# A hand-planned instruction order, replanned with one more dependence and two longer products

## The chip, the core and the metric

The kernel runs on one core of a Trainium2 chip. The core has four compute engines that each work through a queue of their own in order: TensorE (PE in the profile, its weight loads PEld), VectorE (DVE), ScalarE (ACT) and GpSimd (POOL); SyncE (SP) only issues DMAs here. An instruction waits, and everything behind it on its engine with it, until semaphores say that its data are there and that the tile it writes is free. The metric is the device time of one execution in microseconds (us).

## What is computed

Two stages in float32. The first is an attention with sketched features, for 4 batches of 4 heads, 1088 positions, 32 dimensions; S1 and S2 are 8 x 32:

```python
a = einsum('rd,bhsd->bhsr', S1, x); b = einsum('rd,bhsd->bhsr', S2, x)
phi(x) = a (outer) b, reshaped to 64 features
kv = einsum('bhsf,bhsd->bhfd', phi(k), v);  z = sum over s of phi(k)
attn = einsum('bhsf,bhfd->bhsd', phi(q), kv) / (einsum('bhsf,bhf->bhs', phi(q), z) + 1e-6)
```

The second takes its 4352 x 128 result x through a network with a rational activation:

```python
h = x @ w_in                      # 128 -> 2048
P = a0 + a1*h + a2*h**2 + a3*h**3
Q = 1 + |b0|*|h| + |b1|*h**2
out = (P / (Q + 1e-6)) @ w_out    # 2048 -> 128
```

## The kernel before, in words

**The attention.** For each batch `keys` transposes k on DVE (L415, L417, into `kT`), multiplies it on PE with the sketches S (L435, into PSUM), copies one half of the result on ACT (L440, `b_sk`), forms the features on DVE (L443, `k_p`) and sums them against v on PE (L454); ACT keeps the result (L473, `kvz`). `queries` does the same for q in pieces of up to 384 positions: DVE transposes (L498, `qT`), and then one of two ways. In the direct way, used for the first two pieces of batch 0, PE multiplies `qT` with SAB, the sketches already repeated for all 64 features: L520 with SAB0 and later L520 with SAB1, into other columns of the same PSUM tile. ACT copies the SAB0 half (L525 or L528, into `a_all`), and DVE multiplies the SAB1 half by the copy (L532 or L535). In the spread way, used for all other pieces, PE makes the plain sketches (L548), ACT copies them (L553, `sk_sb`), SP writes them to DRAM and reads them back repeated (`sk_d`, then `a_all` and `b_all`), and DVE multiplies (L556). Either way PE then multiplies by `kvz` (L589), DVE divides (L598, L602, L605, `x_tok`), PE transposes (L611), and ACT puts the result into `xT` (L618).

**The network.** 4352 tokens are cut into tiles of 256 or 512, each of 16 blocks of 128 hidden features, and the blocks into 29 units of up to 6 blocks (3072 columns). In a unit PE forms h in chunks of 1024 columns (L691) in two PSUM tiles that take turns, ACT takes each chunk out of PSUM (L695), and DVE and ACT compute on the whole unit: DVE |h| (L706), b0 + b1|h| (L711 on DVE or L713 on ACT), its product with |h| (L716); ACT the logarithm (L719) and the exponential of its negative, 1/Q (L722); DVE h/Q (L731) and so on (L734, L737, L740, L749, L752), with a linear term on DVE (L726) or on ACT (L728), and a1 added on DVE (L744) or on ACT (L746). The digit of `MODES` says how many terms of P go through the output matrix separately. In mode 4 there are four terms, 1/Q, h/Q, h^2/Q and h^3/Q, each with a copy of w_out scaled by a0 to a3, and no linear term. In mode 3 there are three, and the linear term a2 + a3*h is multiplied in (L728 or L726, then L737). PE adds the terms up in PSUM (L787, against `w_out`); DVE transposes the sums out (L799) and DMAs store them (L811). The five scaled copies of w_out are made at the start (L391, L393 on ACT; L395, L397 on DVE).

**The order.** The work is cut into 976 steps, each a few instructions on one engine. Every step has a number in `PLACE`; the steps are issued in the order of these numbers, so the table is the order of every engine's queue at once. It comes from a planner outside the kernel; the costs, ranks and slacks that the step calls still carry have no effect here. `ON_ACT` lists the steps that could go to DVE or ACT and go to ACT. `FILLS` gives zero products (L321: an `idle` tile of zeros times itself, 256 columns) ahead of some places. A step's `after` list is only compared with the places; what an instruction waits for follows from the tiles that it reads and writes. Two tiles each named att, out and h are all of PSUM, and 16 tiles t hold the units' columns; each is given in turn to whoever has the next place.

Of the kernel before, what the change touches and what calls it, by code (L numbers as in the profile page):

```python
# [20 lines left out]
def kernel(  # L21
# [38 lines left out]
    PE, DVE, ACTE, POOL, SP = "PE", "DVE", "ACT", "POOL", "SP"  # L60
# [27 lines left out]
    def step(eng, cost, fn, rank, after=(), uses=(), land=None, early=0.0, behind=None, slack=0.0):  # L88
        s = Step()
        s.eng = (ACTE if len(steps) in ON_ACT else DVE) if isinstance(eng, dict) else None  # L90
        s.fn, s.uses = fn, list(uses)
        s.after = [a for a in list(after) + [behind] if a is not None]
        s.place = PLACE[len(steps)]
        for b in s.uses:
            b.left += 1
        steps.append(s)
        return s
# [18 lines left out]
    def act(n, extra=0.0):  # L116
        return 0.04 + 0.000835 * n + extra

    def d_one(n):
        return 0.066 + 0.00104 * n  # L120
# [4 lines left out]
    def d_four(n, ptr):  # L125
# [17 lines left out]
    FILL = 1  # L143
    LATE = 6.96
    Q0B_RANK = -194.15
    GET_SLACK = 1.2
    S_SLACK = (0.0, 1.0)
    V_SLACK = 0.99
    GAP = 0.2
    START = 4.9  # L150
    Q0_PRE = -151.2
    K1_RANK = 0.47
    MODES = '43242333333243333233444244424'
    FIRST_PER = 4
    LAST_PER = (8, 8, 8, 4, 3, 1)
    K0_PARTS = ((0, 1), (1, 4), (4, 6), (6, 8), (8, 9))
# [2 lines left out]
    AB_RANK = -145.0  # L159
# [3 lines left out]
    PERS = (6,)  # L163
    N_T = 16
    PLACE = (
# [48 lines left out]
    )  # L214
    ON_ACT = (
        25, 26, 29, 31, 32, 33, 328, 342, 344, 379, 454, 478, 502, 535, 612, 636, 669, 688, 693, 744, 878,
        889, 914, 932, 951, 953, 960,
    )
    FILLS = {7: 15, 22: 4, 70: 1, 77: 1}
    NW = 5 if '4' in MODES else 3  # L220


# [74 lines left out]
    ab_in = []  # L297
# [71 lines left out]
    st = step(DVE, 0.15, mk_rep, -210, after=s_l)  # L369
# [4 lines left out]
    ab_ps = Buf("out")  # L374
# [1 line left out]
    def mk_ab():  # L376
        nc.tensor.matmul(ab_ps.t[:, 0:6], lhsT=ones, rhs=ab_row, start=True, stop=True)

    st = ab_st = step(PE, 0.11, mk_ab, AB_RANK, after=ab_in, uses=[ab_ps])
    ab_l = step(ACTE, 0.2, lambda: nc.scalar.copy(out=a_sb, in_=ab_ps.t[:, 0:4]), -100, after=[st], uses=[ab_ps])  # L380
    babs = step(ACTE, 0.2, lambda: nc.scalar.activation(out=b_abs, in_=ab_ps.t[:, 4:6], func=ACT.Abs), -100, after=[st], uses=[ab_ps])

# [106 lines left out]
    def queries(b, qb, q_l, c0, c1, rank, how, pre=None, pre2=None, apart=False, early=0.0, size=1):  # L489
# [12 lines left out]
        if how == "direct":  # L502
# [32 lines left out]
                    nc.vector.tensor_mul(out=av(hp), in0=half(hp, n, 2 * n), in1=av(hp))  # L535

            st = step(PE, 0.57 * n / 256, lambda: sketches((0,)), rank if pre is None else pre, after=[tr, sab[0]], uses=[qT] + pair)
            s2 = step(PE, 0.57 * n / 256, lambda: sketches((1,)), rank if pre2 is None else pre2, after=[tr, sab[1]], uses=[qT] + pair)
            st = step(ACTE, act(2 * n) + 0.02 * apart, copies, rank, after=[st], uses=pair + [a])
            ft = step(DVE, d_one(2 * n) + 0.07 * apart, features, rank, after=[st, s2], uses=pair + [a])  # L540
        else:
            sk, c, d, a, bb = (Buf(z) for z in ("att", "sk_sb", "sk_d", "a_all", "b_all"))
# [323 lines left out]
```

## Time and profile before

| | us |
|---|---|
| runs | 266.0, 266.1, 266.26 (median 266.1) |
| the profiled execution | 265.84 |
| its span, first to last instruction | 264.1 |
| granted TensorE clock in the profile | 1.00 |
| PE's last product begins | 259.9 |
| DVE's last instruction ends | 260.7 |
| ACT's last instruction ends | 258.3 |

A row of the timeline gives the start, the duration, the engine, the line, the operation with output and inputs, and how many instructions were merged. In brackets stands how long the engine had been idle, and what ended that. Neighbours on one engine overlap by some 0.1 us in their records, so two rows' starts tell better than a duration what an instruction costs its queue.

### The profile page before, as it was taken

What the parts mean: (1) busy time and instruction counts of PE and PEld (TensorE: products, weight loads), DVE (VectorE), ACT (ScalarE), POOL (GpSimd) and SP (SyncE); (2) the same over time, 40 slices, a digit from 0 to 9 for tenths busy, and PEclk for the clock granted to TensorE, in tenths of its full rate; (3) what the DMA queues carried; (4) which work ended last, traced back from release to release, by engine and by line L of the source; (5) the groups of instructions that cost most, each with busy time, mean ns of one, the idle gap of its engine ahead of it and who ended that gap; (6) DMA issues with size and microseconds to landing.
All of it is one profiled execution on the core that took longest, in us unless ns stands there. A gap on an engine that the chain in (4) does not pass through costs nothing.

```text
span 264.1 us, 4201 instructions
## 1 busy us (share of the span) xinstructions
PE 254.8 (96%) x1641; PEld 141.1 (53%) x1659; DVE 252.4 (96%) x293; ACT 248.5 (94%) x209; POOL 2.7 (1%) x25
## 2 busy tenths in 40 slices
PE   8999999999999999999999999999999999999994
PEld 5767646554544654454444554444444466565683
DVE  3889999999999999999999999999999999999994
ACT  2779999999999999999999999999999999999991
POOL 4000000000000000000000000000000000000000
PEclk9999999999999999999999999999999999999999
DMA  7969344800425347005102530300010110030032
GB/s 199 338 193 241 79 134 128 242 32 0 97 70 178 93 132 163 4 7 129 34 2 80 104 87 21 55 0 0 0 22 2 25 18 0 0 46 0 0 55 40
DMA packets 29063, 20.13 MB, mean 76 GB/s; under 512 B 19316, under 2 KB 24948, under 8 KB 29044
## 3 DMA queue, kind: packets, MB, share of 16 engines
q1 hardware_dynamic: 28352, 19.24, 29.2%
q10 hardware_dynamic: 692, 0.62, 0.8%
q8 instruction: 13, 0.21, 0.4%
q14 instruction: 6, 0.05, 0.1%
HBM read 16.65 MB, written 3.21 MB: 75 GB/s over the span
## 4 chain that ended last, share of the span: by engine, by line
ACT 51%; PE 30%; DVE 10%; issue 8%; POOL 0%; ACTq 0%; POOLq 0%
PE h_ps L691 14%; ACT ln L719 13%; ACT t L722 13%; ACT t L695 11%; PE out_ps L787 7%; ACT t L728 6%; ACT t L713 3%; DVE t L734 2%; DVE t L737 2%; PE att_ps L589 1%; DVE t L731 1%; PE att_ps L548 1%; DVE t L716 1%; PE att_ps L321 1%; PE att_ps L435 1%
## 5 line engine op out<-in xcount | busy, mean ns | idle before, releaser
L691 PE MATMUL h_ps<-xT,w_in_sb 128*128 128x512 f32 (+1 forms) x320 | 127.2, 534 | 1.2 <-ACT xT L618 0.7
L787 PE MATMUL out_ps<-t,w_out 128*128 128x512 bf16 (+1 forms) x480 | 97.8, 344 | 1.9 <-issue 1.1
L691 PEld LDWEIGHTS h_ps<-xT,w_in_sb 128*128 128x128 f32 x320 | 58.8, 190 | 45.4 <-issue 33.3
L787 PEld LDWEIGHTS <-w_out 128*128 128x128 bf16 x498 | 47.2, 98 | 49.5 <-issue 17.9
L695 ACT CAST t<-h_ps 128x1024 bf16<-128x1024 f32 (+1 forms) x69 | 69.4, 1053 | 0.5 <-PE h_ps L691 0.4
L719 ACT ACTIVATE ln<-t 128x3072 f32<-128x3072 bf16 (+4 forms) x29 | 65.5, 2257 | 0.3 <-DVE t L716 0.2
L722 ACT ACTIVATE t<-ln 128x3072 bf16<-128x3072 f32 (+4 forms) x29 | 65.4, 2254 | 0.2
L731 DVE TENSOR_TENSOR t<-t,t 128x3072 bf16<-128x3072 bf16 (+4 forms) x29 | 40.4, 1397 | 0.0
L716 DVE TENSOR_TENSOR t<-t,t 128x3072 bf16<-128x3072 bf16 (+4 forms) x29 | 40.4, 1392 | 0.0
L728 ACT ACTIVATE t<-t,a_sb 128x3072 bf16<-128x3072 bf16 (+2 forms) x13 | 33.3, 2574 | 0.4 <-PE out_ps L787 0.4
L734 DVE TENSOR_TENSOR t<-t,t 128x3072 bf16<-128x3072 bf16 (+3 forms) x23 | 32.7, 1425 | 0.1
L706 DVE TENSOR_SCALAR t<-t 128x3072 uint16<-128x3072 uint16 (+4 forms) x29 | 22.4, 773 | 0.6 <-ACT t L695 0.4
L711 DVE TENSOR_SCALAR t<-t,b_abs 128x3072 bf16<-128x3072 bf16 (+3 forms) x24 | 22.3, 928 | 0.0
L737 DVE TENSOR_TENSOR t<-t,t 128x3072 bf16<-128x3072 bf16 (+1 forms) x13 | 21.6, 1661 | 0.0
L589 PEld LDWEIGHTS att_ps<-kvz,a_all 128*64 128x64 f32 x288 | 9.9, 137 | 4.2 <-issue 2.3
L589 PE MATMUL att_ps<-kvz,a_all 128*64 128x66 f32 x288 | 11.3, 225 | 0.0
L752 DVE TENSOR_TENSOR t<-t,t 128x1024 bf16<-128x1024 bf16 (+3 forms) x10 | 11.2, 1124 | 0.0
L556 DVE TENSOR_TENSOR a_all<-a_all,b_all 128x768 f32<-128x768 f32 (+2 forms) x11 | 9.6, 871 | 0.0
L713 ACT ACTIVATE t<-t,b_abs 128x2048 bf16<-128x2048 bf16 (+3 forms) x5 | 9.0, 1809 | 0.1
L443 DVE TENSOR_TENSOR k_p<-att_ps,b_sk 128x768 f32<-128x768 f32 x9 | 8.5, 949 | 0.0
L454 PEld LDWEIGHTS att_ps<-v_sb,k_p 128*64 128x64 f32 x216 | 6.8, 138 | 2.1 <-issue 1.4
L740 DVE TENSOR_TENSOR t<-t,t 128x3072 bf16<-128x3072 bf16 (+3 forms) x6 | 7.7, 1282 | 0.0
(75 smaller groups left out, 145.9 us busy)
## 6 DMA issues: line engine op xcount, KB each, us to landing
a_all<-sk_d SPq DMA_DIRECT2D x6, 384.0 KB
b_all<-sk_d SPq DMA_DIRECT2D x12, 192.0 KB
kq<-in_k_dram SPq DMA_DIRECT2D x3, 544.0 KB
kq<-in_q_dram SPq DMA_DIRECT2D x3, 544.0 KB
a_all<-sk_d SPq DMA_DIRECT2D x4, 320.0 KB
b_all<-sk_d SPq DMA_DIRECT2D x8, 160.0 KB
v_sb<-in_v_dram SPq DMA_DIRECT2D x4, 288.0 KB
v_sb<-in_v_dram SPq DMA_DIRECT2D x4, 256.0 KB
```

Source lines behind the costliest of these rows:

```text
L589: nc.tensor.matmul(nd.t[x:x + 64, o:o + 2 * KW], lhsT=(av(c)[:, o0 + x:o0 + x + 64] if how == "direct" else q_p.t[:, c * n + o0 + x:c * n ...
L691: nc.tensor.matmul(h.t[:, cols[x] - cols[x0]:cols[x + 1] - cols[x0]], lhsT=w_in_sb[:, f * 128:(f + 1) * 128], rhs=xT[:, xpos(t0):xpos(t0) ...
L695: nc.scalar.copy(out=hh.t[:, cols[x0]:cols[x1]], in_=h.t[:, 0:cols[x1] - cols[x0]])
L706: nc.vector.tensor_scalar(out=u.t[:, :n].bitcast(U16), in0=hh.t[:, :n].bitcast(U16), scalar1=0x7FFF, scalar2=None, op0=AX.bitwise_and)
L716: nc.vector.tensor_mul(out=y.t[:, :n], in0=w.t[:, :n], in1=u.t[:, :n])
L719: nc.scalar.activation(out=ln.t[:, :n], in_=y.t[:, :n], func=ACT.Ln, bias=1.0 + 1e-6)
L722: nc.scalar.activation(out=r.t[:, :n], in_=ln.t[:, :n], func=ACT.Exp, scale=-1.0)
L728: nc.scalar.activation(out=p.t[:, :n], in_=hh.t[:, :n], func=ACT.Identity, scale=a3, bias=a2)
L731: nc.vector.tensor_mul(out=s.t[:, :n], in0=hh.t[:, :n], in1=r.t[:, :n])
L734: nc.vector.tensor_mul(out=(hh if mode == 3 else p).t[:, :n], in0=hh.t[:, :n], in1=s.t[:, :n])
L737: nc.vector.tensor_mul(out=hh.t[:, :n], in0=p.t[:, :n], in1=hh.t[:, :n])
L787: nc.tensor.matmul(o[0].t[:, :bl[x][1]], lhsT=w_sb[y_][:, bl[x][2], :], rhs=src.t[:, cols[x]:cols[x + 1]], start=(o[1] == 1), stop=(o[1] = ...
```

## The change

`PLACE` is new nearly throughout. Beside it five things differ:

```diff
-    GET_SLACK = 1.2
+    GET_SLACK = 1.15
-    MODES = '43242333333243333233444244424'
+    MODES = '43242333333243333233444244423'
-        0, 3, 1, 8, 4, 5, 10, 2, 9, 18, 13, 71, 16, 17, 11, 6, 7, 14, 19, 21, 15, 29, 33, 30, 80, 46, 91,
+        2, 3, 0, 15, 4, 5, 7, 1, 16, 22, 10, 66, 23, 21, 8, 6, 11, 12, 19, 18, 13, 26, 27, 32, 79, 41, 101,
...
-        25, 26, 29, 31, 32, 33, 328, 342, 344, 379, 454, 478, 502, 535, 612, 636, 669, 688, 693, 744, 878,
-        889, 914, 932, 951, 953, 960,
+        25, 27, 29, 31, 32, 33, 328, 342, 344, 379, 454, 478, 502, 535, 612, 636, 669, 688, 693, 744, 878,
+        889, 914, 932, 951, 953, 960, 965,
-    FILLS = {7: 15, 22: 4, 70: 1, 77: 1}
+    FILLS = {11: 15, 14: 3, 63: 1, 78: 1}
...
-    st = ab_st = step(PE, 0.11, mk_ab, AB_RANK, after=ab_in, uses=[ab_ps])
+    st = ab_st = step(PE, 0.38, mk_ab, AB_RANK, after=ab_in, uses=[ab_ps])
...
-            s2 = step(PE, 0.57 * n / 256, lambda: sketches((1,)), rank if pre2 is None else pre2, after=[tr, sab[1]], uses=[qT] + pair)
             st = step(ACTE, act(2 * n) + 0.02 * apart, copies, rank, after=[st], uses=pair + [a])
+            s2 = step(PE, 0.57 * n / 256, lambda: sketches((1,)), rank if pre2 is None else pre2, after=[tr, sab[1], st], uses=[qT] + pair)
```

In instructions: the last unit (256 columns) goes from mode 4 to mode 3, which adds one L728 on ACT and takes away one L787; four zero products ahead of the first key products become three; of the w_out copy scaled by a1, ACT makes the other half than before, and DVE the half that ACT made. All else is order. At the start, PE's order was L520 with SAB0, L520 with SAB1, then the key products of the later parts (L435, L454); it becomes L520 with SAB0, L435 twice, one L454, then L520 with SAB1. On ACT, L525 now comes ahead of the w_out copy L393 instead of behind it. On SP, the first half of w_in now comes ahead of the k of batch 1, and some loads and puts exchange places. Behind the start, DVE's and PE's queues differ in most places, ACT's in fewer.

94 rows, old and new, of the table PLACE are left out of this document.

## The prediction

> **What bounds the kernel.** The profiled execution took 265.84 us: a span of 264.1 and 1.7 around it. The median of the runs shown is 266.1, 0.26 more, so I work from 265.84 and add 0.26 at the end. I read the page's busy times first, then its slices, the chain that ended last, and the timeline of 0 to 62 us engine by engine.
>
> ```profile
> PE 254.8 (96%) x1641; PEld 141.1 (53%) x1659; DVE 252.4 (96%) x293; ACT 248.5 (94%) x209; POOL 2.7 (1%) x25
> ...
> PE   8999999999999999999999999999999999999994
> ...
> DVE  3889999999999999999999999999999999999994
> ACT  2779999999999999999999999999999999999991
> ...
> ACT 51%; PE 30%; DVE 10%; issue 8%; POOL 0%; ACTq 0%; POOLq 0%
> ```
>
> Three engines are full at once, and the chain hops between all three, so no work of one hides behind another for long. What an order can change is idle time alone. DVE's idle time: 4.34 before its first instruction, rows of 0.55, 0.15, 0.30, 0.54, 0.21 and 0.18 up to 20 us, then only 0.25, 0.19, 0.20, 0.41 and 0.36 in the other 240 us. Behind 20 us there is 1.4 to win on DVE, before it about 1.9, and no more. The start looks like this:
>
> ```profile
> 6.73 0.70 PE L520 MATMUL att_ps<-qT,SAB 64*128 64x256 f32 x4
> 7.89 0.97 PE L520 MATMUL att_ps<-qT,SAB 64*128 64x256 f32 x4 [0.46 <-ACT a_all L528]
> 8.62 0.76 DVE L535 TENSOR_TENSOR a_all<-att_ps,a_all 128x256 f32<-128x256 f32 x2 [0.55 <-PE att_ps L520]
> 9.63 1.15 ACT L391 ACTIVATE w_out<-ln,a_sb 128x1024 bf16<-128x1024 f32 x1
> 12.54 1.05 ACT L393 CAST w_out<-ln 128x1024 bf16<-128x1024 f32 x1
> 13.48 0.59 ACT L525 COPY a_all<-h_ps 128x512 f32<-128x512 f32 x1
> 14.12 0.70 PE L520 MATMUL h_ps<-qT,SAB 64*128 64x256 f32 x4 [0.62 <-ACT a_all L525]
> 15.30 0.29 ACT L553 COPY sk_sb<-att_ps 128x160 f32<-128x160 f32 x1 [1.22 <-PE att_ps L548]
> ```
>
> The reader is to see that PE waits twice for the copies of the first query products (0.46 and 0.62), although they lie in other columns of the same PSUM tile: the dependence is real already, and the changed step list only names it. DVE (0.55) and ACT (1.22) wait behind the same places.
>
> **The start.** In the changed order PE does key products while the copies run. On before's rows: three zero products instead of four let the first key products begin at about 5.59 (5.80 less one spacing of 0.21). The L520 pair of 6.73 comes at about 6.5, its copies end at about 7.9, and PE meanwhile does the L435 and L454 groups that stood at 8.79 to 9.5, so the wait of 0.46 is covered by that work. ACT's L391 is now asked for at about 8.1. Its row started at 9.63 without a wait, so its data came somewhere between; if as late as 9.63, the small copy behind it and a DVE product stay where they were, and at 11 us the gain is only 0.2 to 0.3. It comes back: ACT's L393 (0.94 from start to start) no longer stands ahead of L525, which can run at about 12.45 instead of 13.48. So the 0.62 goes, the L520 of 14.12 comes at 13.15, L532 at 14.1 instead of 14.95, and the first L691 at 15.65 instead of 16.53. L691 waits for its half of w_in_sb; SP now issues that ahead of the k of batch 1, one 0.5 MB load earlier. ACT's first L695 then starts at 17.6 instead of 18.56. DVE by 20 us is about 1.05 ahead, ACT 0.95, PE 0.88. **Start: -0.9.** Bounds: -0.25 (the L391 wait is not made good) to -1.2.
>
> The loads and the spread of the later queries move in SP's queue, some behind puts that wait for ACT. On before's rows each has at least 5.7 us between its last forerunner and its use (the q of batch 2 least, as before), and the second half of b_all, now behind the next puts, about 5. I cost this at nothing; without that cover it would be up to 2.8, the longest wait for b_all in SP's own list.
>
> **The middle.** The ACT order is nearly unchanged up to 60 us; DVE's and PE's are not, and two edits spend the gain:
>
> ```profile
> 43.25 1.93 ACT L695 CAST t<-h_ps 128x1024 bf16<-128x1024 f32 x2
> 44.35 1.75 DVE L740 TENSOR_TENSOR t<-t,t 128x3072 bf16<-128x3072 bf16 x1
> 46.10 1.07 DVE L726 TENSOR_SCALAR t<-t,a_sb 128x3072 bf16<-128x3072 bf16 x1
> 51.59 0.51 ACT L618 COPY xT<-att_ps 128x384 f32<-128x384 f32 x1
> 52.16 3.70 PE L691 MATMUL h_ps<-xT,w_in_sb 128*128 128x512 f32 x8 [0.40 <-ACT xT L618]
> 56.62 0.96 DVE L706 TENSOR_SCALAR t<-t 128x3072 uint16<-128x3072 uint16 x1 [0.25 <-ACT t L695]
> ```
>
> At 44.35 DVE did L740, and L726, which needs the last L695 of 43.25 (ended 45.18), came at 46.10, 0.92 later than its data. The changed order has L726 ahead of L740, so DVE asks at 44.35 less its gain of 1.05, 43.3, while ACT's data, 0.95 earlier, come at about 44.25. **DVE waits about 0.95** and has then nothing left of its gain. What is queued behind it: L706, L598 and L740, and through them the next L719. At 52 us the copy L618 moves behind one more L695 (0.90 from start to start), so in spite of ACT's gain it still ends at about 52.1; PE, there 0.24 further in its own work than before, asks at 51.5 and **waits about 0.65 instead of 0.40**. So at 53 us DVE is at 0, PE at -0.24, ACT at -0.95. Then ACT's gain pays: the 0.25 at 56.62 is a wait for ACT's L695 and goes. **DVE at 57 us: -0.25.**
>
> From 60 to 250 us the orders differ throughout. I compared, for each L719 with its L716, each L731 with its L722 and each L695 with its L691, how much work stands ahead of it on its own engine and on the other, by the rows' spacings, before and after. The tightest pairs are alike: ACT has at most 4.40 us less work ahead of an L719 than DVE has through its L716, 4.27 after; DVE at least 4.25 more ahead of an L731 than ACT through its L722, 4.14 after; PE at least 9.11 more ahead of the L691 that reuses a PSUM tile than ACT ahead of its L695, 8.88 after. One pair is worse, the third last L695 (by 0.8 against its L691), where ACT has 2 us to spare to the end. So I expect waits of the same size as before's, at other places. The waits of before behind 57 us that can go are 0.19, 0.20, 0.41 and 0.36 on DVE (1.16 in all), and ACT's lead, which DVE's waits use up, allows 0.70 of it. Bounds: 0 and -0.70; I take half, **-0.35**. PE's products change kind 175 times instead of 180; what one change costs beyond its work is between 0 and 0.16 (the "issue" waits in PE's rows), so 0 to -0.8 on PE, taken as 0, since DVE and ACT are as full.
>
> **The end.** The last unit (256 columns) goes from mode 4 to mode 3: one L787 of 0.11 us less, one L728 on ACT more, about 0.5 (the 256-column L713 took 0.60, 0.51 from start to start). ACT was through at 258.30 and DVE's last product at 259.87, so the 0.5 delays L746 by that much, and L749 behind it, only if ACT's lead is gone. Taken as 0; bounds -0.1 and +0.5.
>
> **Sum:** the start's 0.9 is spent on DVE at L726, -0.25 remains at 57 us, -0.35 comes behind it, 0 at the end: -0.6, so 265.24 for a profiled execution and **265.5** as a median.
>
> **A rule that speaks against fewer zero products.**
>
> ```profile
> 1.29 3.41 PE L321 MATMUL att_ps<-idle 128*128 128x256 bf16 x15
> ...
> 250.90 9.30 PE L787 MATMUL out_ps<-t,w_out 128*128 128x256 bf16 x82 [0.27 <-ACT t L722]
> ```
>
> The zero products are 256 columns wide, as the last L787 are, and take 0.21 apart (3.41 less the last one's own 0.42, over 14), those 0.11: TensorE runs at half rate at the start, though the profile's granted clock reads 1.00 from the first slice on. The L435 of 5.80 (0.69 for 16) run at the rate of later ones, so the full rate came by then, 4.7 us after the first zero product. If the fourth zero product were needed for that, and the half rate lasted as long again, PE's rows from 5.8 to 10.5 would take twice as long: up to 4.5 us, of which 1.0 is covered by waits that go; half of it, as DVE and ACT are still idle there 2 of 5 us, gives 1.8 against a gain of 0.6, so 267.3. Against it: in the changed order PE is at work from 5.59 on, so nothing idles for the want of it.
>
> The Trainium skill ("TensorE: Matmul & The Clock Gate", Part 1) says that the array starts at half clock and is released after a window of about 3.4 us of sustained activity that runs freely, counted in time and not in products. By that rule the removed product costs nothing while other products take its place, and by a rule that counted products it would; the spacings of 0.21 and 0.11 agree with its two rates, and no run so far shows its window.
>
> **Rivals.**
> 1. *The start's gain lasts.* If ACT's evacuations come early enough that L726 and L691 wait less, 0.9 stays, and fewer changes of kind give 0.2: 264.7, median **265.0**. For it: ACT is 0.95 ahead. Against: L726 stands ahead of its data by more than that.
> 2. *The gain is given back.* The waits move and sum to before's: 265.84, median **266.1**. For it: three engines above 94%, any one that loses 0.9 sets the end. This is also what is left if the step list's new dependence changes nothing but names.
> 3. *ACT becomes the last engine, and slower.* At 132 us the changed order puts an L691 0.45 us ahead of the end of the L695 that frees its PSUM tile, which stands behind an L728 of 2.85; at before's 208.78 the same kind of wait was 0.39. With ACT's lead PE doesn't notice. If ACT has lost its lead by then (its L719 at 71 us has only 0.09 to spare against DVE, which stands at -0.25), PE loses 0.45 there and the added L728 its 0.5 at the end: 265.84 + 0.95 = 266.8, median **267.05**. It decides if ACT's lead at 130 us is under 0.2 and the start's gain is gone with it.
> 4. *The half rate lasts*, 267.3, median **267.55**.
>
> **Chances.** Forecast 0.31, rival 1 0.23, rival 2 0.30, rival 3 0.13, rival 4 0.03. What a measurement of this kernel can tell from no change is about 0.2%, 0.53 us. Faster by more: most of the forecast's case (0.26 of 0.31, as -0.6 is near the bound) and rival 1, 0.49; within it: rival 2 and the rest of the forecast, 0.35; slower: 0.16. The range reaches from rival 1 with the start's larger bound (264.6) to the lower part of rival 3 (266.7). The likeliest case's own range is 265.1 to 265.9.
>
> **What would show it.** The first L691 at 15.5 to 15.8, and no 0.46, 0.55, 0.62 or 1.22 in the start's rows; if the first L691 is later than 16.2, the start is wrong. A wait of 0.7 to 1.2 in front of DVE's first L726 of 3072 columns, for L695; if it is under 0.3, rival 1. PE waiting 0.5 to 0.8 for L618 near 51 us. DVE's idle behind 20 us: 1.0 to 1.8 in all, for before's 1.4. A wait of PE for L695 near 131 us and an ACT that ends less than 1 us ahead of DVE speak for rival 3. Zero products and first key products further than 0.11 and 0.06 apart after 6 us speak for rival 4.

## The result and the profile after

The changed kernel takes **265.5 us** (median of 10 runs, 265.03 to 266.51), the kernel before 266.17 (10 runs, 265.87 to 266.46): a ratio of 0.9975, interval 0.9963 to 0.9987, that is 0.67 us less. The profiled execution took 265.17, its span is 263.4, and the column of the granted clock reads 1.00 throughout. The forecast of 265.5 was met; not all of its steps were, as will be seen.

Busy times and the chain that ended last, from the page of the changed kernel:

```profile
PE 255.6 (97%) x1657; PEld 140.5 (53%) x1657; DVE 252.4 (96%) x293; ACT 249.2 (95%) x210; POOL 2.8 (1%) x25
...
PE 49%; ACT 31%; DVE 11%; issue 5%; DMA 3%; DVEq 0%; ACTq 0%
```

PE now has the larger share of the chain (49% for 30%), and a load has entered it (DMA 3%). Of the kernel before, two rows serve as marks, the first product of the network and the last transpose:

```profile
16.53 1.99 PE L691 MATMUL h_ps<-xT,w_in_sb 128*128 128x256 f32 x8
260.24 0.45 DVE L799 STREAM_TRANSPOSE out_sb<-out_ps 128x256 f32<-128x256 f32 x1 [0.36 <-PE out_ps L787]
```

The timeline of the changed kernel, start and end:

```profile
5.58 0.69 PE L435 MATMUL h_ps<-S,kT 128*64 128x64 f32 x16 [0.35 <-DVE S L355]
9.45 1.15 ACT L391 ACTIVATE w_out<-ln,a_sb 128x1024 bf16<-128x1024 f32 x1 [1.33 <-DMA ln<-in_moe_w_out_dram]
10.71 0.42 DVE L443 TENSOR_TENSOR k_p<-h_ps,b_sk 128x256 f32<-128x256 f32 x1 [0.63 <-ACT b_sk L440]
11.19 0.45 PE L454 MATMUL out_ps<-v_sb,k_p 128*64 128x64 f32 x8 [0.56 <-DVE k_p L443]
12.75 0.59 ACT L525 COPY a_all<-h_ps 128x512 f32<-128x512 f32 x1 [0.28 <-PE h_ps L520]
13.46 0.70 PE L520 MATMUL h_ps<-qT,SAB 64*128 64x256 f32 x4
14.64 0.29 ACT L553 COPY sk_sb<-att_ps 128x160 f32<-128x160 f32 x1 [0.25 <-PE att_ps L548]
15.81 1.99 PE L691 MATMUL h_ps<-xT,w_in_sb 128*128 128x256 f32 x8
259.53 0.45 DVE L799 STREAM_TRANSPOSE out_sb<-out_ps 128x256 f32<-128x256 f32 x1 [0.48 <-PE out_ps L787]
```

The waits of 0.46, 0.55 and 0.62 are gone, and of the 1.22 ahead of L553 0.25 is left. In their place ACT's L391 stands 1.33 until the first half of w_out has landed; behind it stands the small copy L440, and so L443 (0.63) and L454 (0.56). L525 no longer stands behind L393, and the first L691 comes at 15.81 instead of 16.53, **0.72 earlier**. The last L799 begins at 259.53 instead of 260.24, 0.71 earlier. Within 0.01, nothing was won or lost in the 244 us between.

### The profile page after: what moved, and what is told of

Its sections match the earlier page's. It is cut to its first block, busy times and chain, and to the rows that moved or that the text cites. A ratio compares the mean times of both kernels' runs of the same rounds, so it can differ in the third digit from the quotient of the medians.

```text
span 263.4 us, 4224 instructions
## 1 busy us (share of the span) xinstructions
PE 255.6 (97%) x1657; PEld 140.5 (53%) x1657; DVE 252.4 (96%) x293; ACT 249.2 (95%) x210; POOL 2.8 (1%) x25
## 4 chain that ended last, share of the span: by engine, by line
PE 49%; ACT 31%; DVE 11%; issue 5%; DMA 3%; DVEq 0%; ACTq 0%
PE h_ps L691 24%; PE out_ps L787 16%; ACT t L695 9%; ACT ln L719 9%; ACT t L722 7%; ACT t L728 4%; PE att_ps L589 3%; DVE t L734 3%; DVE t L731 3%; PE att_ps L454 2%; DMA ln<-in_moe_w_out_dram 2%; DVE t L752 2%; DMA kq<-in_k_dram 1%; PE att_ps L548 1%; DVE t L716 1%
## 5 line engine op out<-in xcount | busy, mean ns | idle before, releaser
L691 PE MATMUL h_ps<-xT,w_in_sb 128*128 128x512 f32 (+1 forms) x320 | 127.4, 534 | 1.1 <-ACT t L695 0.7
L787 PE MATMUL out_ps<-t,w_out 128*128 128x512 bf16 (+1 forms) x497 | 100.7, 346 | 0.5 <-DVE t L731 0.4
L691 PEld LDWEIGHTS h_ps<-xT,w_in_sb 128*128 128x128 f32 x320 | 58.8, 190 | 44.5 <-issue 32.5
L787 PEld LDWEIGHTS <-w_out 128*128 128x128 bf16 x497 | 47.2, 98 | 50.3 <-issue 18.9
L695 ACT CAST t<-h_ps 128x1024 bf16<-128x1024 f32 (+1 forms) x69 | 69.2, 1041 | 0.7 <-PE h_ps L691 0.5
L728 ACT ACTIVATE t<-t,a_sb 128x3072 bf16<-128x3072 bf16 (+3 forms) x14 | 34.2, 2442 | 0.0
L706 DVE TENSOR_SCALAR t<-t 128x3072 uint16<-128x3072 uint16 (+4 forms) x29 | 22.6, 778 | 0.6 <-ACT t L695 0.5
L737 DVE TENSOR_TENSOR t<-t,t 128x3072 bf16<-128x3072 bf16 (+2 forms) x14 | 21.9, 1572 | 0.0
L752 DVE TENSOR_TENSOR t<-t,t 128x1024 bf16<-128x1024 bf16 (+2 forms) x9 | 10.9, 1214 | 0.0
L556 DVE TENSOR_TENSOR a_all<-a_all,b_all 128x768 f32<-128x768 f32 (+2 forms) x11 | 9.7, 878 | 0.0
L443 DVE TENSOR_TENSOR k_p<-att_ps,b_sk 128x768 f32<-128x768 f32 x9 | 8.5, 952 | 0.4 <-ACT b_sk L440 0.3
L454 PEld LDWEIGHTS att_ps<-v_sb,k_p 128*64 128x64 f32 x216 | 6.8, 138 | 2.7 <-issue 1.8
```

Source lines behind the costliest of these rows:

```text
L691: nc.tensor.matmul(h.t[:, cols[x] - cols[x0]:cols[x + 1] - cols[x0]], lhsT=w_in_sb[:, f * 128:(f + 1) * 128], rhs=xT[:, xpos(t0):xpos(t0) ...
L695: nc.scalar.copy(out=hh.t[:, cols[x0]:cols[x1]], in_=h.t[:, 0:cols[x1] - cols[x0]])
L706: nc.vector.tensor_scalar(out=u.t[:, :n].bitcast(U16), in0=hh.t[:, :n].bitcast(U16), scalar1=0x7FFF, scalar2=None, op0=AX.bitwise_and)
L728: nc.scalar.activation(out=p.t[:, :n], in_=hh.t[:, :n], func=ACT.Identity, scale=a3, bias=a2)
L787: nc.tensor.matmul(o[0].t[:, :bl[x][1]], lhsT=w_sb[y_][:, bl[x][2], :], rhs=src.t[:, cols[x]:cols[x + 1]], start=(o[1] == 1), stop=(o[1] = ...
```

## The experiments

The most useful reading of the study splits each profile at the first L691, the first product of the network. The sixth column is the length from there to the last L799; the profiled time is 5.59 to 5.66 more than the start of that L799 in every row. "L391" is the start of the first copy of w_out; each ratio is against runs of the kernel before on the same chip in the same set.

| kernel | first L391 | first L691 | L691 less L391 | last L799 | length | median | ratio to before (interval) |
|---|---|---|---|---|---|---|---|
| before | 9.63 | 16.53 | 6.90 | 260.24 | 243.71 | 266.17 | |
| changed | 9.45 | 15.81 | 6.36 | 259.53 | 243.72 | 265.5 | 0.9975 (0.9963-0.9987) |
| e1 changed start | 10.20 | 16.55 | 6.35 | 260.25 | 243.70 | 265.77 | 0.9991 (0.9974-1.0008) |
| e2 changed rest | 9.68 | 16.58 | 6.90 | 260.27 | 243.69 | 266.31 | 1.0008 (0.9998-1.0018) |
| e3 no zero products | 9.51 | 18.02 | 8.51 | 261.68 | 243.66 | 267.25 | 1.0044 (1.0031-1.0057) |
| e4 small copy first | 10.04 | 15.98 | 5.94 | 259.76 | 243.78 | 264.8 | 0.9959 (0.9947-0.9970) |
| e5 L740 first | 9.45 | 15.80 | 6.35 | 259.39 | 243.59 | 265.23 | 0.9974 (0.9962-0.9985) |
| e6 last unit mode 4 | 9.37 | 15.72 | 6.35 | 259.49 | 243.77 | 265.62 | 0.9992 (0.9963-1.0020) |
| e7 SAB1 alone | 9.41 | 16.31 | 6.90 | 260.01 | 243.70 | 266.06 | 1.0008 (0.9988-1.0028) |
| e8 L525 alone | 9.56 | 16.20 | 6.64 | 259.91 | 243.71 | 265.64 | 0.9979 (0.9957-1.0000) |
| e9 DVE +0.9 | 9.38 | 15.74 | 6.36 | 259.55 | 243.81 | 265.56 | 0.9980 (0.9967-0.9993) |
| e10 ACT +0.9 | 10.27 | 16.62 | 6.35 | 261.33 | 244.71 | 266.46 | 1.0013 (1.0003-1.0024) |
| e11 PE +1.0 | 10.64 | 17.00 | 6.36 | 261.54 | 244.54 | 266.35 | 1.0012 (0.9997-1.0027) |
| e12 e4, second L391 later | 10.16 | 16.14 | 5.98 | 260.24 | 244.10 | 265.33 | 0.9972 (0.9956-0.9989) |

**e1 and e2: start and rest apart.** The two orders hold the same steps in their first 128 places but for two, so each start can be joined to the other's rest.

```
e1: PLACE = changed order[0:128]   + order of before for the other steps   (last unit mode 4)
e2: PLACE = order of before[0:128] + changed order for the other steps     (last unit mode 3)
```

> The first 128 places (about 22 us) in the changed order with its zero products, all steps behind them in the order of before, last unit in mode 4. Theory A, the start's gain lasts (0.4 us of DVE idle and 0.7 us of PE and ACT position won in the first 20 us): median 265.5 to 265.7, that is 0.45 to 0.7 under before. Theory B, the start's gain is spent at the later waits and the gain of the change comes from the order behind 22 us: within 0.2 of before (266.2). Theory C, both parts give about half: 265.75 to 265.95.

> The first 128 places in the order of before with its zero products, all steps behind them in the changed order, last unit in mode 3. Theory A: within 0.2 of before (266.2). Theory B: 265.4 to 265.7. Theory C: 265.75 to 265.95. If start and rest only work together, because the rest was laid out for engines that are ahead by the changed start, then this one is slower than before, 266.4 to 267.

The changed rest behind the old start (e2) gains nothing: 243.69 for 243.71, and 1.0008. Theory A holds there, and B falls. The median of e1, 265.77, lies in C's range, but its interval, from 0.9974 to 1.0008, reaches over A's range and over no gain at all. So it does not decide between A and C; that e2 gained nothing speaks against C, and the profile of e1 does too: the old rest behind the changed start takes the same 243.70, and the first L691 stands 6.35 behind L391, as in the changed kernel. It came late because the load did:

```profile
10.20 1.15 ACT L391 ACTIVATE w_out<-ln,a_sb 128x1024 bf16<-128x1024 f32 x1 [1.99 <-DMA ln<-in_moe_w_out_dram]
```

SP's queue is the same in e1 and the changed kernel up to this load, so 9.45 and 10.20 are two landings of the same order. In the nine profiles that have the changed start with its zero products L391 began between 9.37 and 10.64, each time behind a wait for this load.

**e7 and e8: the two parts of the start apart**, each on the kernel before.

```
e7 PE : L520(SAB0), L435, L435, L454, L520(SAB1), L435, L454 ...   was L520(SAB0), L520(SAB1), L435, L435, L454 ...
e7 DVE: L443, L443, L535                                           was L535, L443, L443
e8 ACT: L553, L525, L393                                           was L553, L393, L525
```

> The kernel before with one part of the change alone: the L520 with SAB1 stands behind three key products' groups and one L454 on PE, and L535 behind two more L443 on DVE, as in the changed kernel. Theory, ACT's L391 waits for its data and holds the key chain up, so that PE's gain of 0.5 at 8 us is lost again by 11 us and L393 is still ahead of L525: first L691 within 0.15 of 16.53, median 266.0 to 266.3. Rival, the removed waits of 0.46 and 0.55 are the gain of the change: first L691 at 15.9 to 16.1 and 265.5 to 265.8.

> The kernel before with the other part alone: ACT's L525 ahead of the w_out copy L393. Theory, this is what gives the start's gain: the wait of 0.62 of PE's L520 goes, first L691 at 15.7 to 16.0 instead of 16.53, median 265.4 to 265.7, as much as the whole change. Rival, the start's gain is eaten by DVE's and PE's next waits in the order of before (the 0.54 before L532 goes, and the loads of w_in and k come no earlier): 265.9 to 266.2.

e7: no gain in time (1.0008), as the theory said; the first L691 came at 16.31, 0.07 further from 16.53 than expected, because L391 could begin at its landing, 9.41. The length of 6.90 behind L391 is that of before: PE's early products don't shorten it. e8: the wait of 0.62 goes and some time with it (0.9979, with an interval that just reaches 1), but L691 comes at 16.20, not at 15.7 to 16.0. In e8's timeline:

```profile
12.85 0.59 ACT L525 COPY a_all<-h_ps 128x512 f32<-128x512 f32 x1 [0.29 <-PE h_ps L520]
13.49 0.70 PE L520 MATMUL h_ps<-qT,SAB 64*128 64x256 f32 x4
16.20 1.99 PE L691 MATMUL h_ps<-xT,w_in_sb 128*128 128x256 f32 x8 [0.23 <-DMA w_in_sb<-in_moe_w_in_dram]
```

L691 waits 0.23 for its half of w_in, which in the order of before is loaded behind the k of batch 1. Without that wait the length behind L391 would be 6.41, close to 6.36. So the 0.72 between the two profiles consists of 0.18 from L391 (9.63 to 9.45, free to begin at the landing because of the SAB1 part) and 0.54 from the order of L525 and L393, of which some 0.23 also needs the earlier load of w_in. That load by itself was not tried. The 0.18 belongs to a run with an early landing: in e2, with the start of before, L391 also waited for the load (0.23, to 9.68), and in a run like that the SAB1 part wins nothing. The 0.54 stays: e1 has 6.35 behind its late L391, e2 has 6.90.

**e5 and e6: two steps of the prediction undone.**

```
e5 DVE: L556, L740, L726, L706, L598    was L556, L726, L706, L598, L740 (at 43 us)
e6 MODES: ...4244424 , ON_ACT without 965    was ...4244423
```

> The changed kernel with one step moved back: DVE's L740 of 43 to 46 us stands ahead of L726 and L706 again, as before. The prediction's step (L726 ahead of its data takes DVE's gain away) would make this 0.2 to 0.7 faster than the changed kernel, 264.8 to 265.3. The theory from the trace of the changed kernel, where L726 followed the L556 of 42.96 without a wait of 0.15 or more, because DVE came to 44 us only some 0.3 to 0.5 ahead: no difference, 265.4 to 265.7.

> The changed kernel with the last unit in mode 4 again: L728 of 256 columns goes, one L787 more, L752 in place of L737. The prediction's step (the mode of the last unit is worth nothing): within 0.15 of the changed kernel, 265.4 to 265.7, with ACT's end 0.5 earlier and nobody behind it. Rival, the shorter last chain (one product less behind DVE's last product) is part of the gain: 265.7 to 265.9.

First the changed kernel, then e5:

```profile
42.07 1.95 ACT L695 CAST t<-h_ps 128x1024 bf16<-128x1024 f32 x2
42.96 0.95 DVE L556 TENSOR_TENSOR a_all<-a_all,b_all 128x768 f32<-128x768 f32 x1
44.06 1.08 DVE L726 TENSOR_SCALAR t<-t,a_sb 128x3072 bf16<-128x3072 bf16 x1
```

```profile
42.94 0.95 DVE L556 TENSOR_TENSOR a_all<-a_all,b_all 128x768 f32<-128x768 f32 x1
43.80 1.75 DVE L740 TENSOR_TENSOR t<-t,t 128x3072 bf16<-128x3072 bf16 x1
```

Start to start, the L556 is followed after 1.10 in the changed kernel and after 0.86 in e5: the wait before L726 is 0.24, not 0.95. DVE asked at 43.82, for a forecast of 43.3, and the data were there at 44.02, for a forecast of 44.25. Undone, the length shrinks by 0.13, which is hardly more than the other kernels of the first ten rows differ among themselves (243.66 to 243.78), and the ratio changes by nothing (0.9974 for 0.9975). The median, 265.23, lies below what the trace's theory expected and within the other's range, but it was taken in another set of runs; against the runs of before beside it there is no gain. e6: 243.77 for 243.72, so the mode of the last unit is worth nothing, as forecast; its ratio (0.9963 to 1.0020) is too wide to add to that.

**e3: the zero products.**

```
-    FILLS = {11: 15, 14: 3, 63: 1, 78: 1}
+    FILLS = {63: 1, 78: 1}
```

> The changed kernel without the 15 zero products at the start and the 3 ahead of the first key products (one zero product remains at 1.1 us). Theory, the half rate is lifted only by products that run: the first key products and the first L520 (begin at 5.6 and 6.5 in the changed kernel) take twice as long from start to start until some 4 us of work are done, PE loses about 1 to 1.5 us by 10 us, part of it covered by its waits of 0.35 and 0.56: 0.3 to 1.0 slower than the changed kernel, 265.8 to 266.5. Rival, the rate is lifted by time from the start of the program alone: products 0.06 and 0.11 apart as in the changed kernel and 265.4 to 265.6.

It costs more than expected: 267.25, 1.0044 of before. Timeline of e3, then its L454 counted in stretches of half a microsecond (the first column is the stretch, its length and the busy time follow):

```profile
5.50 1.12 PE L435 MATMUL h_ps<-S,kT 128*64 128x64 f32 x16 [0.44 <-DVE S L355]
7.07 1.23 PE L520 MATMUL att_ps<-qT,SAB 64*128 64x256 f32 x4
```

```profile
12.00:12.50 0.50, 0.50 (x14) 1.00 1.01 401
12.50:13.00 0.50, 0.50 (x16) 1.00 1.04 419
13.00:13.50 0.50, 0.50 (x22) 1.00 1.00 400
```

The first key products take 1.12 instead of 0.69, the first L520 1.23 instead of 0.70, and the half rate ends only at about 13 us, 7.5 behind the first key product. The column of the granted clock reads 1.00 on both sides of that point. The first L691, at 18.02, is 2.21 later than in the changed kernel. So the theory has the cause right and both sizes too small: the half rate ended 7.5 us, not some 4, behind the first key product, and the price was 1.75, not 0.3 to 1.0. It is near the 1.8 that the prediction gave rival 4, but that was worked out for one zero product less and 4.7 us more of half rate; here 18 zero products are missing.

**e4 and e12: the wait for w_out.**

```
e4  ACT: L440, L391, L391, L473, L553, L525, ...        was L391, L440, L391, L473, L553, L525, ...
e12 ACT: L440, L391, L473, L553, L525, L391, L553, L618, L391, L391, L393
```

> The changed kernel with one step moved: ACT's 32 column copy L440 goes ahead of the first w_out copy L391, which waits 1.33 for its data. Theory, this wait holds up the key chain: the wait of 0.63 of DVE's L443 at 10.71 and of 0.56 of PE's L454 at 11.19 go or fall under 0.2, the first L691 comes at 15.3 to 15.5 instead of 15.81, and the median is 0.2 to 0.4 under the changed kernel's, 265.1 to 265.3. Rival, the key chain is not what sets the first L691 (ACT's L391 pair and L525 set it, and L391 now begins 0.1 to 0.2 later): first L691 at 15.7 to 16.0, time unchanged within 0.15.

> The kernel of e4 (small copy L440 ahead of the first L391) with the second L391 moved behind L618, so that L473 and L525 no longer wait behind two copies of w_out. Theory, the first L691 sets the time (begin of the last L799 = first L691 + 243.7, time = that + 5.6): it comes 5.3 to 5.9 behind the first L391 instead of 5.94, and the median is 264.4 to 264.8. Rival, the loads of q and w_out set the first L691 now: same as e4, 264.7 to 265.0; or the delayed L391 makes the first L695 late and the length behind the first L691 grows past 244.0.

e4 **beats the kernel before**: 264.8 (5 runs), 0.9959 of it (0.9947 to 0.9970). Against the changed kernel it was not run side by side, and the two intervals overlap by a little (0.9963 to 0.9970). The profiled execution took 265.39, the longest of the five, and shows what comes next. Timeline of e4:

```profile
9.18 0.19 ACT L440 COPY b_sk<-h_ps 128x32 f32<-128x32 f32 x1 [0.96 <-PE h_ps L435]
10.04 2.19 ACT L391 ACTIVATE w_out<-ln,a_sb 128x1024 bf16<-128x1024 f32 x2 [0.68 <-DMA ln<-in_moe_w_out_dram]
11.21 0.77 DVE L498 STREAM_TRANSPOSE qT<-kq 128x256 f32<-128x256 f32 x2 [0.71 <-DMA kq<-in_q_dram]
```

The 0.63 and 0.56 are gone, and the key chain no longer hangs on w_out. Next in line is the load of q (0.71). L691 came at 15.98, not at 15.3 to 15.5, with a late landing of w_out: at the changed kernel's 6.36 behind L391 it would have come at 16.40 (10.04 and 6.36), so 0.42 is won in this run. e12 is a miss, and the causes that its rivals name both show: its first L691 gained nothing on e4's (5.98), since q still sets it (it comes 4.77 behind the L498 that waited for q in both), and the length grew to 244.10, since with three copies of w_out in a row the first L695 starts at 18.62, right behind the last of them and not waiting for PE, and an L618 behind it keeps PE waiting, in the timeline of e12:

```profile
11.37 0.77 DVE L498 STREAM_TRANSPOSE qT<-kq 128x256 f32<-128x256 f32 x2 [0.89 <-DMA kq<-in_q_dram]
21.06 0.57 PE L435 MATMUL att_ps<-S,kT 128*64 128x64 f32 x12 [0.48 <-ACT xT L618]
```

**e9, e10, e11: which engine sets the 243.7.** In the changed kernel an L706 (DVE) and an L695 (ACT) are issued twice, which changes no value, and nine zero products are added on PE, each between 124 and 130 us.

```
e9, e10: for _ in range(2 if s.place == 504 else 1): s.fn()      (503 in e10)
e11:     FILLS = {11: 15, 14: 3, 63: 1, 78: 1, 506: 9}
```

> The changed kernel with one DVE instruction issued twice, the L706 of 3072 columns at 128 us (0.9 more on DVE, same result). In eight kernels so far the last L799 began 243.6 to 243.8 behind the first L691, in whichever of the two orders. Theory P, PE's queue sets that length and DVE has slack: it stays at 243.6 to 244.0. Theory D, DVE sets it as much as PE: 244.4 to 244.7.

> The changed kernel with one ACT instruction issued twice, the L695 at 125 us (0.9 more on ACT, same result). Theory P: the length from the first L691 to the last L799 stays at 243.6 to 244.0. Theory A, ACT sets it as much as PE: 244.4 to 244.7.

> The changed kernel with nine zero products of 0.11 more on PE at 127 us, between two L787. Theory P, PE's queue is what is full behind the first L691: the length to the last L799 is 244.6 to 244.9, 0.9 to 1.1 more. Rival, DVE's or ACT's waits cover it: under 244.2.

By the starts of the rows behind them, the added work holds its engine up by 0.96 on DVE, 0.97 on PE and 1.13 on ACT. DVE's costs 0.09: theory D falls. PE's costs 0.82, a little under the expected 0.9; ACT's costs 0.99, and so theory P is right on DVE and wrong on ACT. DVE makes its delay good only slowly: of the 0.96, some 0.8 is left at 131 us, 0.46 at 175 us and 0.1 at 206 us. How ACT's work reaches PE, in e10's timeline and then at the same place in the changed kernel:

```profile
133.41 1.98 PE L691 MATMUL h_ps<-xT,w_in_sb 128*128 128x512 f32 x4 [0.81 <-ACT t L695]
```

```profile
131.64 1.93 PE L691 MATMUL h_ps<-xT,w_in_sb 128*128 128x512 f32 x4
```

## Why the prediction came true, point by point

**The start: right in kind, 0.72 for 0.9.** L391 was asked for at 8.12 and did wait, nearly to the bound given (9.45 for 9.63), and the loss was regained where forecast: L525 at 12.75 (12.45 forecast), L520 at 13.46 (13.15), L691 at 15.81 (15.65). One detail is right by accident. The first key products began at 5.58 (5.59 forecast), but behind a wait of 0.35 for S; the removed zero product did not set it.

**DVE's lead: wrong.** The forecast had DVE 1.05 ahead at 20 us. Its idle up to 22 us went from 6.27 (4.34 and the six rows) to 5.87 (4.24, 0.20, 0.63, 0.30, 0.17, 0.33): 0.40. It lost 0.63 to the L440 that stood behind L391, which PE and ACT made good by L525, and another 0.33 at 21.17 for an L695. I took a lead from the starts of rows that have different work ahead of them in the two orders.

**The middle: the step that failed.** "DVE waits about 0.95" at L726 was 0.24, under the 0.3 that the prediction had named as the sign of rival 1, and PE's wait for L618 was 0.35 instead of 0.65, less than before. And a wait of DVE need not be a loss of time at all: with the 0.24 undone (e5) the ratio is the same, and 0.96 more on DVE at 128 us cost 0.09 (e9). That "no work of one hides behind another for long" was wrong for DVE there. The same holds for the **-0.35** from DVE's later waits: those of 0.25, 0.19, 0.20 and 0.41 went, others of 0.29 and 0.19 came, the last one, ahead of the final L799, grew from 0.36 to 0.48, and the length stayed at 243.7 in both orders (e1, e2). The forecast spent 0.65 of the start at L726 and earned 0.35 later; neither happened. The number is right by luck: the loss and the later gain, neither of which came, and a start taken too large nearly cancel, as -0.9 + 0.65 - 0.35 = -0.6 lies near -0.72. **Rival 1, that the start's gain lasts, tells what happened**, at 0.72 rather than its 0.9 and the 0.2 for fewer changes of kind. PE's 175 for 180 changes of kind are worth nothing that shows (the length is equal to 0.02).

**The end** was taken as 0 and is, as far as e6 shows; ACT's last instruction ended 0.5 earlier than before (257.77) in spite of the added L728.

**Rival 3 did not come, and its place is real.** ACT kept its lead, as PE and ACT gained the same 0.72. In the changed kernel the L691 at 131.64 finds its tile free; with ACT 0.9 behind it waits 0.81 (e10), where 0.45 had been worked out for a lost lead of 0.95.

**Rival 4 and the rule.** Its time has a slip: 265.84 + 1.8 - 0.6 is 267.04, so 267.3 is already the median, and 267.55 counts the 0.26 twice. (By its own terms the range would likewise begin at 264.7, not 264.6.) In the changed kernel's own profile the zero products went to the full spacing at about 4.1 us, before the missing one would have run. But in three of the nine profiles with three zero products ahead of the keys (e5, e9, e10), and in none of four with four, the first key products ran at half rate, in e5:

```profile
5.05 0.82 PE L321 MATMUL out_ps<-idle 128*128 128x256 bf16 x3
5.80 1.12 PE L435 MATMUL h_ps<-S,kT 128*64 128x64 f32 x16
```

It cost nothing: the first L691 stayed 6.35 or 6.36 behind L391, since L391 waits for its load anyhow. Whether the fourth zero product keeps this away is not settled by so few, but the traces speak against it. They hold records of the clock's changes, which the views don't print. In these the full rate begins at 4.04 in the changed kernel, 5.69 in that of before, 6.80 to 6.93 in e5, e9 and e10, and 13.09 in e3, and lasts a whole number of stretches of 3.413 us (74 to 76). Counted back by one such stretch, the last boundary before the full rate lay at 0.63 in the changed kernel, and at 3.39 to 3.52 in e5, e9 and e10, where the zero products running since 1.10 had not been enough. So the moment seems to hang on where these stretches fall, and not on a third or fourth zero product; that is argued from the fourteen profiles, and no run tested it.

The Trainium skill ("TensorE: Matmul & The Clock Gate", Part 1) has the release follow one busy window of some 3.4 us, free-running. The stretches of 3.413 us agree with it, and so do releases at 2.9 us (changed kernel) to 5.8 us (e10) from the first zero product, if a window need not be busy from its start. The 7.5 us of narrow f32 products in e3 are more than two such windows, and there the measurement decides.

**What stays open.** Why w_out's first half lands up to 1.3 us apart was not tested; that this makes the spread of the changed kernel's runs (265.03 to 266.51) is argued from the table, not shown run by run. The split of the start's gain rests on one profile of each kernel, and the earlier load of w_in was not tried alone. The slack of the three engines was measured at 124 to 130 us only (at least 0.8 for DVE there).

## What to carry to other kernels

Split a full pipeline at the first instruction of its long, full part and compare the length behind that point between orders: here it was 243.59 to 243.78 in ten kernels made of two quite different orders, and everything that the replanned order won had been won before it. Waits of an engine are worth counting only if work added on that engine moves the end; a doubled instruction tells that, for its place in the program, in one run. And an early load that a queue's head waits for should have nothing urgent behind it: with one small copy moved ahead of it the ratio to the kernel before was 0.9959, for 0.9975 without, though the two intervals still overlap.

## What the runs showed of the hardware

- PE's half rate at the start is not in the column of the granted clock, which reads 1.00 there; it is seen in the spacings: zero products 0.21 apart against 0.11, f32 key products 1.12 for 16 against 0.69. By the trace's clock records it ended between 4.04 and 6.93 us in the thirteen profiles where 16 zero products ran from 1.10 on, and at 13.09 in e3, where after one zero product the work began with a transpose at 4.80 and key products at 5.50.
- The same first load of w_out, behind the same queue, let L391 begin anywhere from 9.37 to 10.64 in nine profiles.
- A wait of 0.24 (L726) stands in no bracket: the records of L556 (to 43.91) and L726 (from 44.06) are only 0.15 apart, since neighbouring records overlap where nothing waits. The distance from start to start shows it (1.10 against 0.86).
